# Strassen output product in a pooled-attention MLP kernel: which queue carries loads and stores, how x is normalised, and when pooling starts

## The chip, the cores and the metric

The kernel runs on one core of one Trainium2 chip. The metric is the device time of that core in microseconds. A core has TensorE (PE in the profile; its weight loads are PEld), VectorE (DVE), ScalarE (ACT), GpSimd (POOL) and SyncE (SP). SyncE, ScalarE and GpSimd can issue DMAs; the data is moved by 16 DMA engines. All engines work through their own instruction streams in order and wait for each other by semaphores.

## The reference

Attention with pooled keys and values, then an MLP without biases. Batch 8, 8 heads, 576 positions, head size 64, hence 4608 tokens of 512 features; hidden size 2048. All inputs and the output are float32.

```python
k_p = k.reshape(B, H, S // 8, 8, D).mean(axis=3)       # 72 pooled keys
v_p = v.reshape(B, H, S // 8, 8, D).mean(axis=3)
attn = softmax(q @ k_p.T / sqrt(D))
x = (attn @ v_p) as [B * S, H * D]                     # 4608 x 512
h = x @ w_in                                           # 4608 x 2048
g = h - tanh(h)
out = g @ w_out                                        # 4608 x 512
```

## The kernel before

The tokens are taken in nine groups g of 512 (TG), while the attention works in eight batches of 576 tokens. Attention runs ahead of the MLP: during group g of the MLP, the scores and the attention product of batch nb = g + 1 are computed and the inputs of batch nn = g + 2 are loaded and pooled. The order of the instructions is written out by hand; each engine executes its part in that order.

**Hidden layer of a group.** Eight steps p (`h_pair`, the last one as two `h_one`). Each multiplies xT with two 128-column slices of w_in into two PSUM banks (L538), ScalarE takes the tanh (L550), VectorE subtracts it (L551) into Gt. During these steps VectorE also forms sums of Gt, P (`sum_p`, L559) and Q (`sum_q`, L564).

**Output product of a group.** Strassen's scheme with seven products n of half-size blocks, each in two halves u (u = 0..13), accumulated in two PSUM banks, C1 = 6 and C2 = 7 (L594). Between them `after_product` copies or combines partial results: ScalarE copies C1 (L632, L638, L645), VectorE writes quarters of the output tile O (L634, L643, L648), GpSimd subtracts m4 = O − m45 (L639), and VectorE forms the differences Dg of Gt (`sum_d`, L569), which the sixth and seventh products read. The last quarter is copied after the loop (L993). O is one buffer [128, 4, 512]: tiles 0 and 1 are token rows 0..255 of the group, tiles 2 and 3 rows 256..511.

**Attention inside the output product.** Scores of batch nb at u = 0..4 (`scores`, L349, exponential L368). At u = 6, 7, 8, 9, 11 one block of 128 tokens each (`av`): per half of the heads, three matmuls (L396) into one PSUM bank, a reciprocal of the four denominators (L413), and a product (L414) into x_sb, a pool of five buffers. Banks 2 to 5, 0 and 1 take turns for this; the next group's `h_pair` uses them again, beginning with 0 and 1. x_sb is transposed into xT by DMA (L443). Blocks that belong to the next group are transposed at once, later ones (`late`) in the next group, before its output product. xT is a ring of three groups.

**Queues before the change.** SyncE's queue carries, in this order in each group: the transpose of the pooled keys (L332, at p = 0), five transposes of q (L205, each after a ScalarE cast of q, L192), the loads of batch nn (k 2 DMAs, v 5, q 2; L137 to L170), the `late` transposes of x and those of the first blocks of batch nb (L443). GpSimd's stream carries: pooling of k and v of batch nn (`pool_k`, `pool_v`, from u = 6; L248 to L291), placing the transposed keys (`k_place`), the stores of the previous group's four tiles (`store_tile`, L615, emitted at p = 0), and m4 (L639). The loads wait for buffers: k_raw and v_raw have two each, used by batches in turn; q_raw has one, free after the third ScalarE cast of the batch before.

The stores of the last group are issued after the loop on SyncE (`store`, L611); the last product is done for each of the two row tiles apart, copied to O (L1004), and stored in turn on SyncE and ScalarE (L1006). A tile of 128 rows can consist of two segments in the output, which then are two DMAs; in the last group all four tiles do.

Of the kernel before, what the change touches and what calls it, by code (L numbers as in the profile page):

```python
# [8 lines left out]
FP32 = mybir.dt.float32  # L9
# [19 lines left out]
NT = 5  # L29
# [13 lines left out]
def kernel(  # L43
# [89 lines left out]
            nc.vector.tensor_copy(out=out, in_=in_)  # L133
        evac_n[0] += 1

    def load_main(src, dst, b, t0, t1):
        return nc.sync.dma_start(out=dst[:, t0:t1, :], in_=src[b, 0:128, t0:t1, :])  # L137

    def load_left(src, dst, b, eng=nc.sync):
        return [  # L140
            eng.dma_start(out=dst[32 * t : 32 * t + LO, NM, :], in_=src[b, 128:PR, t, :])
            for t in range(NM)
        ]

    def load_dense(src, dst, b, eng=nc.sync):
        return eng.dma_start(
            out=dst[0 : NM * LO, NM, :], in_=src[b, 128:PR, :, :]
        )

    def load_k(b):  # L150
        return [
            load_main(k_pairs, k_raw[b % 2], b, 0, NM),
            load_dense(k_pairs, k_raw[b % 2], b),
        ]

    def load_v(b):
        return [load_main(v_pairs, v_raw[b % 2], b, 0, NM)] + load_left(
            v_pairs, v_raw[b % 2], b
        )

    def load_q_tail(b, t, eng):
        eng.dma_start(
            out=t[:QT, :, R, :], in_=q[b, :, QA:S, :].rearrange("h p d -> p h d")
        )

    def load_q(b, tail=True):
        if b not in q_raws:
            q_raws[b] = raw.tile([128, H, R + 1, D], FP32, name="q_raw", tag="q_raw")
        t = q_raws[b]
        nc.sync.dma_start(  # L170
            out=t[:, :, 0:R, :], in_=q[b, :, 0:QA, :].rearrange("h (p j) d -> p h j d", j=R)
        )
        if tail:
            load_q_tail(b, t, nc.sync)

    qTs = {}
    kdups = {}
# [60 lines left out]
    def halves(n, b):  # L238
        return ((0, n),) if b < 2 else ((0, n // 2), (n // 2, n))

    def pool_k(b, eng, t0=0, t1=NT, mid=()):
        r = k_raw[b % 2].rearrange("p t (j d) -> p t j d", d=D)[:, t0:t1, :, :]
        if b not in kdups:
            kdups[b] = work.tile([128, NT, 2, D], BF16, name="kd", tag="kd")
        kd = kdups[b][:, t0:t1, :, :]
        n = t1 - t0
        for ta, tb in halves(n, b):
            first = eng.tensor_tensor(  # L248
                out=r[:, ta:tb, 0:4, :], in0=r[:, ta:tb, 0:4, :], in1=r[:, ta:tb, 4:8, :], op=ALU.add
            )  # L250
        for c in mid:
            load_w2(c)
        eng.tensor_tensor(  # L253
            out=r[:, :, 0:2, :], in0=r[:, :, 0:2, :], in1=r[:, :, 2:4, :], op=ALU.add
        )
        eng.tensor_tensor(  # L256
            out=kd,
            in0=r[:, :, 0:1, :].to_broadcast([128, n, 2, D]),
            in1=r[:, :, 1:2, :].to_broadcast([128, n, 2, D]),
            op=ALU.add,  # L260
        )
        return first
# [158 lines left out]
    def new_x():  # L421
        return work.tile([128, 2, 4, D], BF16, name="x_sb", tag="x_sb", bufs=5)

    def av(b, blk, alloc, by_dma):
        x_sb = new_x()
        for half in range(2):
            av_half(b, blk, half, x_sb, alloc)
        if by_dma:
            if b * S + blk * 128 < (b + 1) * TG:
                x_dma_transpose(b, blk, x_sb)  # L430
            else:
                late.append((b, blk, x_sb))
        return x_sb
# [132 lines left out]
        )  # L566

    def sum_d(a, b):
        nc.vector.tensor_tensor(  # L569
            out=Dg[:, a:b, :, :],  # L570
            in0=Gt[:, a:b, :, 0:HT],
            in1=Gt[:, a:b, :, HT:TG],
            op=ALU.subtract,
        )
# [28 lines left out]
    def chain(g, bk):  # L603
        if g == NG - 1 and bk == C1:
            return PS[:, 2:4, 0:HD]
        return PS[:, bk, :].rearrange("p (t n) -> p t n", t=2)

    def store(g, th, c0=0, c1=DM):
        for tt in range(2):
            for r0, r1, dst in out_segments(g * TG + th * HT + tt * 128, 128):  # L610
                nc.sync.dma_start(out=dst[:, c0:c1], in_=O[r0:r1, 2 * th + tt, c0:c1])  # L611

    def store_tile(g, tb):
        for r0, r1, dst in out_segments(g * TG + tb * 128, 128):
            nc.gpsimd.dma_start(out=dst, in_=O[r0:r1, tb, :])  # L615

    def sh(c, off):
        return slice(c.start + off, c.stop + off)
# [8 lines left out]
        (C1, lambda k, c: Dg[:, k, 1, c], w2s[:, 2, :, :]),  # L627
    ]

    def after_product(g, n):  # L630
        if n == 0:
            nc.scalar.copy(out=m4, in_=chain(g, C1))  # L632
        if n == 1:
            nc.vector.tensor_tensor(out=O[:, 2:4, 0:HD], in0=chain(g, C2), in1=m4, op=ALU.add)  # L634
            sum_d(0, 2)
            sum_d(2, 4)
        if n == 2:
            nc.scalar.copy(out=m45, in_=chain(g, C1))  # L638
            nc.gpsimd.tensor_tensor(out=m4, in0=O[:, 2:4, 0:HD], in1=m45, op=ALU.subtract)  # L639
            sum_d(4, 6)  # L640
            sum_d(6, 8)
        if n == 3:
            nc.vector.tensor_tensor(out=O[:, 0:2, HD:DM], in0=m4, in1=chain(g, C2), op=ALU.subtract)  # L643
        if n == 4:
            nc.scalar.copy(out=m451, in_=chain(g, C1))  # L645
            nc.vector.tensor_tensor(out=m451, in0=m451, in1=m45, op=ALU.subtract)
        if n == 5:
            nc.vector.tensor_tensor(  # L648
                out=O[:, 2:4, HD:DM], in0=m451, in1=chain(g, C2), op=ALU.subtract
            )  # L650
# [288 lines left out]
    for g in range(1, NG):  # L939
        nb = g + 1 if g + 1 < B else None  # L940
        nn = g + 2 if g + 2 < B else None
        for p in range(NP - 1):
            c = p if g > 1 else p - 1
            if nb is not None and 0 <= c < 3:
                q_cast_part(nb, c)
            h_pair(g, p, (0, 2, 4, 6, 0, 2, 4)[p], p % 2)
            if g == 1 and p < 4:
                w_sum(w2s[:, 0, :, :], b11, b22, ALU.add, k0=2 * p, k1=2 * p + 2)
            if 3 <= p < 6:
                sum_p(2 * p - 6, 2 * p - 4)  # L950
            if nb is not None and p == 0:
                k_dma_transpose(nb)
                k_place(nb, nc.gpsimd.tensor_copy)
            if g > 1 and p == 0:
                for tb in range(4):
                    store_tile(g - 1, tb)
            if nb is not None and 0 <= c < 3:
                q_dma_transpose(nb, 2 * c, min(2 * c + 2, R + 1))
            if nb is not None and c == 2:
                if nn is not None:  # L960
                    load_k(nn)
                    load_v(nn)
                    load_q(nn)
        h_one(g, NP - 1, 1, 0, 2)
        h_one(g, NP - 1, 0, 1, 3)
        sum_p(6, 8)
        sum_q(0, 4)
        sum_q(4, 8)
        while late:
            x_dma_transpose(*late.pop(0))  # L970
        ps_a = Banks(2, 3, 4, 5, 0, 1)
        for u in range(14):
            n, half = u // 2, u % 2
            bk, lhs, rhs = products[n]
            if n == 6 and g == NG - 1:
                break
            product(g, bk, lhs, rhs, 4 * half, 4 * half + 4, n < 2)
            if half:
                after_product(g, n)
                if g == 1 and n in (1, 2):  # L980
                    w_sum(w2s[:, 2, :, :], b21, b22, ALU.add, k0=4 * n - 4, k1=4 * n)
            if nb is not None:
                if u < NT:
                    scores(nb, u)
                if u == NT:
                    ps_a.n += 2
                if u in (6, 7, 8, 9, 11):
                    av(nb, (6, 7, 8, 9, 11).index(u), ps_b1, True)
                if u == 6 and nn is not None:
                    pool_k(nn, nc.gpsimd)  # L990
                    pool_v(nn, nc.gpsimd)
        if g < NG - 1:
            nc.scalar.copy(out=O[:, 0:2, 0:HD], in_=chain(g, C1))  # L993
    store(NG - 1, 1)
    store(NG - 1, 0, c0=HD)
    bk, lhs, rhs = products[6]
    for tt in range(2):
        product(NG - 1, bk, lhs, rhs, 0, NP, False, (tt,))
        for c0, c1, eng in (
            ((0, HD, nc.scalar.copy),)  # L1000
            if tt == 0
            else ((0, HD // 2, nc.scalar.copy), (HD // 2, HD, nc.vector.tensor_copy))
        ):
            eng(out=O[:, tt, c0:c1], in_=part(NG - 1, C1, tt, c0, c1))  # L1004
        for n, (r0, r1, dst) in enumerate(out_segments((NG - 1) * TG + tt * 128, 128)):
            (nc.sync, nc.scalar)[n % 2].dma_start(out=dst[:, 0:HD], in_=O[r0:r1, tt, 0:HD])  # L1006


# [28 lines left out]
```

The softmax here doesn't subtract the row's maximum and nothing guards it: scores larger than these inputs give would overflow.

## Time and profile before

Three runs: 298.72, 299.71 and 300.87 us; median 299.71. The profiled execution has a span of 300.0 us and a mean granted TensorE clock of 0.988.

| engine | busy us | share of the span |
|---|---|---|
| TensorE, matmul | 281.9 | 94% |
| TensorE, weight load | 179.0 | 60% |
| VectorE | 227.6 | 76% |
| ScalarE | 153.6 | 51% |
| GpSimd | 146.1 | 49% |

How to read it: TensorE's hidden layer and output products are the body of the time, about 29 us for a group; the first group ends at about 56 us, since weights and the first batch must be loaded and prepared. Groups begin their hidden layer at 56.0, 87.25, 118.9, 149.9, 180.5, 209.9, 239.1 and 265.2 us. In the lines of the profile, a row of 40 digits divides the span in slices of 7.5 us; each digit is the busy share in tenths (in the clock row, the granted clock). A wait line tells which engine at which line waited for what, with total, number and longest. A timeline line has start, duration, engine, line, operation, tiles and count; where several instructions are merged, the duration is from the first start to the last end.

### The profile page before, as it was taken

How to read it: one execution, taken by the hardware profiler on the slowest of the kernel's cores; microseconds unless marked ns; L12 is line 12 of the kernel's file. 1: busy time of each engine (PE TensorE's matmuls, PEld its weight loads, DVE VectorE, ACT ScalarE, POOL GpSimd, SP SyncE). 2: the span in 40 equal slices, each digit the busy share in tenths (PEclk: the TensorE clock that was granted, in tenths of full speed). 3: DMA queues.
4: the chain of work that ended last, by engine and by line, in shares of the span. 5: the costliest groups of instructions: out<-in, count | busy, mean ns of one | idle time of the engine just before them, and what ended most of it. 6: DMA issues, size and time to landing. Idle time of an engine off the chain costs nothing.

```text
span 300.0 us, 5470 instructions
## 1 busy us (share of the span) xinstructions
PE 281.9 (94%) x2040; PEld 179.0 (60%) x2040; DVE 227.6 (76%) x400; ACT 153.6 (51%) x244; POOL 146.1 (49%) x166
## 2 busy tenths in 40 slices
PE   7999999999989996999999999999999999999980
PEld 3454455446864685448845874489458845864870
DVE  5658675799977977498969875987898859838940
ACT  4647576586337722566086616660865155235410
POOL 8600909960599259900995199409941040130020
PEclk9999999999999999899999999999999999999997
DMA  7999999949545999399948985799483450030014
GB/s 253 220 213 281 318 236 298 256 79 323 152 86 93 307 296 90 72 267 318 101 92 240 330 125 98 218 351 117 77 184 48 71 149 2 0 120 22 0 27 116
DMA packets 64587, 49.85 MB, mean 166 GB/s; under 512 B 39984, under 2 KB 53296, under 8 KB 64560
## 3 DMA queue, kind: packets, MB, share of 16 engines
q1 hardware_dynamic: 54736, 35.60, 51.8%
q0 software_dynamic: 7248, 12.06, 17.5%
q10 hardware_dynamic: 2576, 1.84, 2.2%
q8 instruction: 16, 0.26, 0.4%
q14 instruction: 11, 0.09, 0.1%
HBM read 36.70 MB, written 9.44 MB: 154 GB/s over the span
## 4 chain that ended last, share of the span: by engine, by line
PE 76%; DMA 10%; DVE 6%; POOL 4%; ACT 1%; issue 1%; ACTq 0%; SPq 0%; POOLq 0%
PE PS L538 34%; PE PS L594 31%; DMA w1b<-in_moe_w_in_dram 4%; PE PS L396 4%; PE PS L520 4%; DMA k_raw<-in_k_dram 4%; PE PS L349 3%; DVE Gt L551 3%; DMA xT<-x_sb 2%; POOL k_raw L248 1%; DVE w2s L577 1%; DVE P L559 1%; DVE x_sb L414 1%; POOL k_raw L253 1%; POOL kd L256 1%
## 5 line engine op out<-in xcount | busy, mean ns | idle before, releaser
L538 PE MATMUL PS<-xT,w1b 128*128 128x512 bf16 x512 | 113.5, 383 | 5.2 <-DMA xT<-x_sb 3.1
L551 DVE TENSOR_TENSOR Gt<-PS,TS 128x1024 bf16<-128x1024 f32 x56 | 68.4, 1221 | 28.2 <-ACT TS L550 28.2
L538 PEld LDWEIGHTS <-w1b 128*128 128x128 f16 x512 | 50.0, 98 | 66.3 <-issue 6.8
L550 ACT ACTIVATE TS<-PS 128x1024 f32<-128x1024 f32 x56 | 57.3, 1024 | 37.2 <-PE PS L538 28.4
L639 POOL TENSOR_TENSOR m<-O,m 128x512 f32<-128x512 f32 x8 | 11.9, 1492 | 98.3 <-ACT m L638 74.7
L414 DVE TENSOR_TENSOR x_sb<-PS,rden 128x256 bf16<-128x256 f32 x72 | 30.6, 425 | 6.6 <-DMA xT<-x_sb 4.2
L594 PE MATMUL PS<-w2s,Dg 128*128 128x256 f16 x256 | 30.2, 273 | 0.0
L615 POOL DMA_DIRECT2D out_dram<-O x44 | 23.6, 545 | 13.4 <-ACT O L993 13.4
L248 POOL TENSOR_TENSOR k_raw<-k_raw 128x512 f32<-128x512 f32 (+2 forms) x13 | 22.0, 1709 | 16.6 <-DMA k_raw<-in_k_dram 16.6
L594 PEld LDWEIGHTS <-Gt 128*128 128x128 bf16 x256 | 24.4, 98 | 5.8 <-DVE Gt L556 0.5
L594 PEld LDWEIGHTS <-P 128*128 128x128 bf16 x256 | 24.5, 98 | 4.7 <-issue 1.4
L594 PEld LDWEIGHTS <-Dg 128*128 128x128 bf16 x256 | 24.5, 98 | 2.8 <-issue 0.2
L368 ACT ACTIVATE E<-PS 128x288 bf16<-128x288 f32 x60 | 21.3, 410 | 7.7 <-PE PS L349 7.6
L559 DVE TENSOR_TENSOR P<-Gt 128x1024 bf16<-128x1024 bf16 x32 | 22.0, 687 | 0.6
L569 DVE TENSOR_TENSOR Dg<-Gt 128x1024 bf16<-128x1024 bf16 x32 | 22.1, 750 | 0.0
L396 PE MATMUL PS<-VB,E 128*128 128x130 bf16 x240 | 20.2, 220 | 0.1
L645 ACT COPY m<-PS 128x512 f32<-128x512 f32 x8 | 4.7, 586 | 29.5 <-PE PS L594 29.5
L267 POOL TENSOR_TENSOR v_raw<-v_raw 128x512 f32<-128x512 f32 (+1 forms) x12 | 19.6, 1654 | 0.0
L396 PEld LDWEIGHTS <-E 128*128 128x128 bf16 x240 | 16.8, 98 | 1.9 <-issue 0.4
L349 PE MATMUL PS<-qT,KB 128*128 128x288 bf16 (+5 forms) x128 | 17.0, 289 | 0.2
L594 PE MATMUL PS<-w2s,Gt 128*128 128x256 f16 x128 | 16.7, 273 | 0.4 <-DVE Gt L556 0.2
L993 ACT COPY O<-PS 128x512 f32<-128x512 f32 x7 | 4.1, 585 | 24.6 <-PE PS L594 24.6
(109 smaller groups left out, 399.1 us busy)
## 6 DMA issues: line engine op xcount, KB each, us to landing
k_raw<-in_k_dram SPq DMA_DIRECT2D x7, 1024.0 KB, 7.3
q_raw<-in_q_dram SPq DMA_DIRECT2D x7, 1024.0 KB, 12.4
v_raw<-in_v_dram SPq DMA_DIRECT2D x7, 1024.0 KB, 11.2
out_dram<-O POOLq DMA_DIRECT2D x32, 128.0 KB, 5.6
out_dram<-O POOLq DMA_DIRECT2D x12, 256.0 KB, 3.6
w1b<-in_moe_w_in_dram POOLq DMA_DIRECT2D x4, 512.0 KB, 14.1
w2b<-in_moe_w_out_dram POOLq DMA_DIRECT2D x4, 512.0 KB, 16.7
out_dram<-O SPq DMA_DIRECT2D x4, 256.0 KB, 4.5
```

The lines of the kernel that those rows point to most:

```text
L248: first = eng.tensor_tensor(out=r[:, ta:tb, 0:4, :], in0=r[:, ta:tb, 0:4, :], in1=r[:, ta:tb, 4:8, :], op=ALU.add)
L349: nc.tensor.matmul(dst[p : p + w], lhsT=KB[b % 2][:, o : o + w], rhs=qTs[b][:, m, c0:c1], start=True, stop=True,)
L368: nc.scalar.activation(out=E[:, t, half * hs : (half + 1) * hs], in_=ps[:, :], func=ACT.Exp, scale=SCALE)
L396: nc.tensor.matmul(ps[:, 2 * n : 2 * n + 2, :].rearrange("p h d -> p (h d)") if n < 2 else ps.rearrange("p (a s) d -> p a s d", s=2)[:, :, ...
L414: nc.vector.tensor_tensor(out=x_sb[:, half, :, :], in0=ps[:, :, 0:D], in1=rden[:, :, :].to_broadcast([128, 4, D]), op=ALU.mult,)
L538: nc.tensor.matmul(dst, lhsT=w1b[:, fb, i * 128 : (i + 1) * 128], rhs=xT[:, fb, c0 : c0 + TG], start=(fb == 0), stop=(fb == NFB - 1),)
L550: nc.scalar.activation(out=t2, in_=PS[:, b0 : b0 + 2, :], func=ACT.Tanh)
L551: nc.vector.tensor_sub(out=Gt[:, p, :, :], in0=PS[:, b0 : b0 + 2, :], in1=t2)
L559: nc.vector.tensor_tensor(out=P[:, a:b, :], in0=Gt[:, a:b, 0, :], in1=Gt[:, a:b, 1, :], op=ALU.add)
L569: nc.vector.tensor_tensor(out=Dg[:, a:b, :, :], in0=Gt[:, a:b, :, 0:HT], in1=Gt[:, a:b, :, HT:TG], op=ALU.subtract,)
L594: nc.tensor.matmul(part(g, bk, tt), lhsT=lhs(k, slice(tt * 128, (tt + 1) * 128)), rhs=rhs[:, k, :], start=(first and k == 0 and (tt == 0 o ...
L615: nc.gpsimd.dma_start(out=dst, in_=O[r0:r1, tb, :])
```

## The change

The change redistributes work between queues and engines; what is computed stays the same.

1. The loads of batch nn in the group loop are issued by GpSimd in place of SyncE.
2. `store_tile` is issued by SyncE in place of GpSimd, tiles 2 and 3 at p = 0 (ahead of the transposes of q), tiles 0 and 1 at p = 3 (behind them).
3. `av_both` normalises both halves of a block at once, over two PSUM banks, with one reciprocal and one product where there were two of each.
4. m4 = O − m45 moves from GpSimd to VectorE and from after the third product to after the fourth.
5. All four `sum_d` follow the second product, and the first instruction of `pool_k` on GpSimd waits for the last of them (`gate`), so that pooling and the differences don't run at the same time.
6. In the last group the two output quarters that are ready after the fourth product are stored then; the third is stored on SyncE and GpSimd; the two row tiles of the last quarter are copied by ScalarE and VectorE, one each, and stored on ScalarE's and SyncE's queues.

```diff
-    def load_main(src, dst, b, t0, t1):
-        return nc.sync.dma_start(out=dst[:, t0:t1, :], in_=src[b, 0:128, t0:t1, :])
+    def load_main(src, dst, b, t0, t1, eng=nc.sync):
+        return eng.dma_start(out=dst[:, t0:t1, :], in_=src[b, 0:128, t0:t1, :])
...
-    def pool_k(b, eng, t0=0, t1=NT, mid=()):
+    def pool_k(b, eng, t0=0, t1=NT, mid=(), dep=None):
...
+            if dep is not None and ta == 0:
+                after([first], dep)
...
+    def av_both(b, blk, x_sb):
+        b0 = ps_a.ids[ps_a.n % len(ps_a.ids)]
+        ps_a.n += 2
+        ps = PS[:, b0 : b0 + 2, 0 : 4 * D1].rearrange("p k (h d) -> p k h d", d=D1)
+        for half in range(2):
+            av_mms(b, blk, half, ps[:, half, :, :])
+        rden = work.tile([128, 2, 4, 1], FP32, name="rden2", tag="rden2")
+        nc.vector.reciprocal(out=rden[:, :, :, :], in_=ps[:, :, :, D:D1])
+        nc.vector.tensor_tensor(
+            out=x_sb[:, :, :, :],
+            in0=ps[:, :, :, 0:D],
+            in1=rden[:, :, :, :].to_broadcast([128, 2, 4, D]),
+            op=ALU.mult,
+        )
...
-        for half in range(2):
-            av_half(b, blk, half, x_sb, alloc)
+        if by_dma:
+            av_both(b, blk, x_sb)
+        else:
+            for half in range(2):
+                av_half(b, blk, half, x_sb, alloc)
...
-    def store(g, th, c0=0, c1=DM):
+    def store(g, th, engs, c0, c1):
         for tt in range(2):
             for r0, r1, dst in out_segments(g * TG + th * HT + tt * 128, 128):
-                nc.sync.dma_start(out=dst[:, c0:c1], in_=O[r0:r1, 2 * th + tt, c0:c1])
+                engs[tt].dma_start(out=dst[:, c0:c1], in_=O[r0:r1, 2 * th + tt, c0:c1])
 
     def store_tile(g, tb):
         for r0, r1, dst in out_segments(g * TG + tb * 128, 128):
-            nc.gpsimd.dma_start(out=dst, in_=O[r0:r1, tb, :])
+            nc.sync.dma_start(out=dst, in_=O[r0:r1, tb, :])
...
         if n == 1:
             nc.vector.tensor_tensor(out=O[:, 2:4, 0:HD], in0=chain(g, C2), in1=m4, op=ALU.add)
-            sum_d(0, 2)
-            sum_d(2, 4)
+            for k in range(0, NP, 2):
+                gate[0] = sum_d(k, k + 2)
         if n == 2:
             nc.scalar.copy(out=m45, in_=chain(g, C1))
-            nc.gpsimd.tensor_tensor(out=m4, in0=O[:, 2:4, 0:HD], in1=m45, op=ALU.subtract)
-            sum_d(4, 6)
-            sum_d(6, 8)
         if n == 3:
+            nc.vector.tensor_tensor(out=m4, in0=O[:, 2:4, 0:HD], in1=m45, op=ALU.subtract)
             nc.vector.tensor_tensor(out=O[:, 0:2, HD:DM], in0=m4, in1=chain(g, C2), op=ALU.subtract)
+            if g == NG - 1:
+                store(g, 1, (nc.sync, nc.sync), 0, HD)
+                store(g, 0, (nc.sync, nc.sync), HD, DM)
...
-            if g > 1 and p == 0:
-                for tb in range(4):
+            if g > 1 and p in (0, 3):
+                for tb in (2, 3) if p == 0 else (0, 1):
                     store_tile(g - 1, tb)
...
-                    load_k(nn)
-                    load_v(nn)
-                    load_q(nn)
+                    load_k(nn, nc.gpsimd)
+                    load_v(nn, nc.gpsimd)
+                    load_q(nn, eng=nc.gpsimd)
...
-                    pool_k(nn, nc.gpsimd)
+                    pool_k(nn, nc.gpsimd, dep=gate[0])
                     pool_v(nn, nc.gpsimd)
...
-    store(NG - 1, 1)
-    store(NG - 1, 0, c0=HD)
+    store(NG - 1, 1, (nc.sync, nc.gpsimd), HD, DM)
     bk, lhs, rhs = products[6]
-    for tt in range(2):
+    for tt, eng in ((0, nc.scalar.copy), (1, nc.vector.tensor_copy)):
         product(NG - 1, bk, lhs, rhs, 0, NP, False, (tt,))
-        for c0, c1, eng in (
-            ((0, HD, nc.scalar.copy),)
-            if tt == 0
-            else ((0, HD // 2, nc.scalar.copy), (HD // 2, HD, nc.vector.tensor_copy))
-        ):
-            eng(out=O[:, tt, c0:c1], in_=part(NG - 1, C1, tt, c0, c1))
+        eng(out=O[:, tt, 0:HD], in_=part(NG - 1, C1, tt))
         for n, (r0, r1, dst) in enumerate(out_segments((NG - 1) * TG + tt * 128, 128)):
-            (nc.sync, nc.scalar)[n % 2].dma_start(out=dst[:, 0:HD], in_=O[r0:r1, tt, 0:HD])
+            (nc.scalar if tt == 0 or n else nc.sync).dma_start(
+                out=dst[:, 0:HD], in_=O[r0:r1, tt, 0:HD]
+            )
```

`load_k`, `load_v` and `load_q` pass the issuing engine on in the same way as `load_main`.

More of the change, by code (lines that the diff above doesn't have):

```diff
@@ L148, in load_dense, with load_k, load_v @@
         )
-    def load_k(b):
+    def load_k(b, eng=nc.sync):
         return [
-            load_main(k_pairs, k_raw[b % 2], b, 0, NM),
-            load_dense(k_pairs, k_raw[b % 2], b),
-        ]
-    def load_v(b):
-        return [load_main(v_pairs, v_raw[b % 2], b, 0, NM)] + load_left(
-            v_pairs, v_raw[b % 2], b
+            load_main(k_pairs, k_raw[b % 2], b, 0, NM, eng),
+            load_dense(k_pairs, k_raw[b % 2], b, eng),
+        ]
+    def load_v(b, eng=nc.sync):
+        return [load_main(v_pairs, v_raw[b % 2], b, 0, NM, eng)] + load_left(
+            v_pairs, v_raw[b % 2], b, eng
         )
@@ L164, in load_q_tail, with load_q @@
         )
-    def load_q(b, tail=True):
+    def load_q(b, tail=True, eng=nc.sync):
         if b not in q_raws:
@@ L169, in load_q @@
         t = q_raws[b]
-        nc.sync.dma_start(
+        eng.dma_start(
             out=t[:, :, 0:R, :], in_=q[b, :, 0:QA, :].rearrange("h (p j) d -> p h j d", j=R)
@@ L173, in load_q @@
         if tail:
-            load_q_tail(b, t, nc.sync)
+            load_q_tail(b, t, eng)
     qTs = {}
@@ L568, in sum_d @@
     def sum_d(a, b):
-        nc.vector.tensor_tensor(
+        return nc.vector.tensor_tensor(
             out=Dg[:, a:b, :, :],
@@ L628 @@
     ]
+    gate = [None]
     def after_product(g, n):
```

## The prediction

> **What bounds the kernel now.** I read the page first: the slices of busy time, then the chain of work that ended last.
>
> ```profile
> span 300.0 us, 5470 instructions
> PE   7999999999989996999999999999999999999980
> PEclk9999999999999999899999999999999999999997
> DMA  7999999949545999399948985799483450030014
> PE 76%; DMA 10%; DVE 6%; POOL 4%; ACT 1%; issue 1%; ACTq 0%; SPq 0%; POOLq 0%
> ```
>
> TensorE is nearly full in all but a few slices, so only its holes can be won back: the slices before 120 us, one slice (120 to 127.5 us) with a lower clock, and the last one. PE's waits between 72 and 290 us and the stretches around 118 us show what these are:
>
> ```profile
> PE PS L538 <- DMA xT<-x_sb: 3.1, 2, 2.3
> PE PS L538 <- DVE x_sb L414: 1.2, 1, 1.2
> 116.64:118.92 2.28, 0.00 (x0) 0.03 (x1) 1.86 (x6) 1.53 (x2) 2.28 (x3) 0.94 0.60 118
> 118.92:120.00 1.08, 1.08 (x3) 0.40 (x4) 0.71 (x3) 0.00 (x0) 1.08 (x1) 0.50 0.73 143
> 120.00:121.00 1.00, 1.00 (x3) 0.29 (x2) 0.00 (x0) 0.00 (x0) 0.92 (x2) 0.50 0.67 131
> 121.00:122.00 1.00, 1.00 (x4) 0.43 (x3) 0.00 (x0) 0.00 (x0) 0.92 (x2) 0.50 0.55 108
> ```
>
> Columns of the last four: stretch, length, busy time of PE, PEld, DVE, ACT, POOL, granted clock, DMA share, GB/s. Three waits stand at the start of a group: 0.86 us at 87.25 (group 2), 2.28 us at 118.92 (group 3), 1.24 us at 180.53 (group 5). After the 2.28 us the clock is 0.50 until 122: group 3's hidden layer takes 15.51 us by the chain, where groups 2 and 4 take 13.99 and 13.97. That makes 1.53 us.
>
> Why is xT late? SyncE's queue, in order of time, in group 2:
>
> ```profile
> 96.10 0.58 SPq L137 DMA_DIRECT2D k_raw<-in_k_dram  x1
> 98.00 2.94 SPq L141 DMA_DIRECT2D v_raw<-in_v_dram  x4
> 100.99 0.55 SPq L170 DMA_DIRECT2D q_raw<-in_q_dram  x1
> 103.76 1.48 SPq L162 DMA_DIRECT2D q_raw<-in_q_dram  x1
> 105.36 12.18 SPq L443 DMA_TRANSPOSE xT<-x_sb  x5
> DMA to landing us min/median/max: 11.5/11.5/11.5
> ```
>
> The loads of the batch after next stand ahead of the transposes of x. The first transpose issued behind them holds SyncE for 4.46 us and lands after 11.5 us, against 2.5 us for one on a quiet queue. Its x_sb buffer therefore comes free late (VectorE's L414 waits 1.0 us for it at 117), and the transpose that group 3 needs is issued at 116.33 though VectorE finished its block at 114.7. It lands at 118.8. Group 5 is the same: the first transpose takes 4.44 us to issue, the piece that the group needs goes at 176.5 and lands 3.8 us later, 180.3. So I read the wait "DVE x_sb L414" at 180.53 as this DMA; a copy happens to end at the same moment.
>
> The end, SyncE's queue and the final scalar line:
>
> ```profile
> 290.45 5.49 SPq L611 DMA_DIRECT2D out_dram<-O  x8
> 296.04 1.17 SPq L1006 DMA_DIRECT2D out_dram<-O  x2
> 292.29 0.51 ACTq L1006 DMA_DIRECT2D out_dram<-O  x1
> ```
>
> The last copy of results ends at 292.26, yet the span lasts to 300.0: eight stores at 0.69 us of issue each stand in one queue ahead of the last two, and the last issue (297.21) needs 2.8 us more.
>
> **What the Trainium skill says.** "DMA: Bandwidth & Descriptors", section Issuing engines are not separate DMA queues: all issuers share the same 16 DMA engines, several issuers save issue time only; its section Queues, rings and completion order adds that an engine takes turns between rings and works through one in order. The 11.5 us landing behind loads agrees with in-order rings; no row of before shows a transpose beside loads on another ring. "SBUF — State Buffer", section SBUF: two separate sides: a GpSimd operation and a VectorE operation with two SBUF inputs exclude each other for a whole instruction. L646 agrees: 0.69 us in the groups without pooling, 0.95 to 2.00 us beside it. "TensorE: Matmul & The Clock Gate", Part 1: the clock halves after an idle window of about 3.4 us. Here 2.28 us was enough, 0.86 and 1.24 us were not.
>
> **The change part by part.**
>
> *Stores at the end.* The eight stores of L611 become twelve, of which eight leave the tail: four (O[2:4], left half) need only L634, done at 283.5, and four (O[0:2], right half) need L643, some 287.3, since the subtraction before it now runs on VectorE (0.69 us there at 288.44) and not on GpSimd (2.01 us, with VectorE waiting 1.16 us). Eight issues of 0.69 from 284 on, the last four from 287.3, are done by 290.1. After L648 (290.42) SyncE has two of the last four (to 291.8) and GpSimd two (0.54 each). The last block is one VectorE copy of 256 elements, 0.43 us like L414, from 291.67 to 292.1; its two stores go at once on SyncE and ScalarE (ScalarE's two earlier ones end at 292.2) and are issued by 292.75. With the same 2.8 us the end is 295.5: **4.5 us less**. Bounds: 3.5 if GpSimd's two land as slowly as its 5.6 us median, 5.0 if nothing queues.
>
> *Loads to GpSimd, stores to SyncE.* GpSimd loses five to eight stores a group (0.54 each, 2.7 to 4.3 us) and L639 (1.5), and gains nine loads. A load's issue is bounded by the 128-row stores, 0.54, and the 512 KB v_raw load, 1.00; I take 0.55 for six small ones and 1.1 for three large: 6.6 us. It stands some 8 us into the group, where the stores stood (95.26, 157.87); behind it is only the next pooling, 12 us later. Its issue costs nothing. The bytes are the same, so what is won is order: the late transposes of x now wait behind stores, not loads, are issued some 12 us into the group instead of 17 to 18, and land by +17 even at the 6.3 us which is the worst landing of a qT transpose. x_sb buffers are free long before they are needed. The store that VectorE's L634 waited 1.55 us for at 106.64 goes about 6 us earlier too.
> Group 5 then starts without a wait: **1.24 us less**. Group 3: VectorE ends block 2 at about 114.4, the transpose goes at 114.7 and lands 2.46 later, 117.15, against PE's end at 116.64: a wait of 0.4 to 0.5, **1.85 us less**, and too short for the clock, **1.53 us less**.
>
> *The price on SyncE.* In groups 2 to 8 two to four stores (0.6 each) go ahead of the five transposes of q. These were done by +9 and the scores need them at +14.9: a delay of 1.2 to 2.4 us fits in the slack of 3 to 5, except that the last ones now run beside the loads. Landing 2.5 (quiet) to 6.3 (worst): +10.5 plus those is +13 to +16.8, so a wait between 0 and 2 us in groups 2 to 5. I take 0.2 each, **0.8 us more**.
>
> *Two-bank normalisation.* Per block two reciprocals (0.17) and two products (0.43), 1.10 us from start to start of blocks, become one reciprocal of 8 (L823, 0.20) and one product of 512 (L824, 0.69), 0.89: 0.2 us less on VectorE, 1.0 per group. It hides beside PE except where the last immediate block decides (groups 2 and 3).
>
> *Subtraction to VectorE, pooling gated.* VectorE gains 0.69 to 2.0 per group, like L646, ahead of L643, ahead of blocks 1 and 2, and of the sixth product, which reuses bank 7: L643 would end 205.3 ± 0.7 in group 5 and the product begins at 205.85. At worst 0.15 us; I take 0.3 in all. The gate makes GpSimd wait for the last difference (202.0 in group 5), which is 1.2 us before its pooling begins today (203.17, behind L639): no loss, and the differences run alone at 0.6 us each. At group 2's start VectorE is the limit: block 2 ends 1.2 later for the subtraction and 0.6 earlier for the pairs, and the transposes follow at 1.2 us each: **0.4 us more**.
>
> Sum: 4.5 + 1.24 + 1.85 + 1.53 − 0.8 − 0.3 − 0.4 = 7.6 us less, 299.71 − 7.6 = **292.1 us**.
>
> **Rivals.**
> All waits gone: the three gaps (4.38), the clock (1.53) and the tail (4.5) give 289.3. For it: groups 6 and 7 already follow without a gap; against it: group 2 is bound by VectorE.
> Contention instead of order: the transposes, now taking turns with loads, land as late as before, and only the tail is won: 299.71 − 4.5 + 0.5 = 295.7. For it: the DMA rows stand at 9 around these times.
> Slower: the scores' transposes of q are held by the loads as those of x were (11.5 instead of 2.5, 9 us less a slack of 4, in four groups, with 1.5 us of halved clock each): 26 − 4.5 more, 321; at a third of it, 304. The same comes if VectorE's paired sums lock GpSimd out of writing its loads, so pooling waits for k. Against it: the transposes of q go mostly before the loads, and GpSimd's stores kept 0.54 us beside these sums.
>
> **How the numbers follow.** 0.6 for my forecast (290.5 to 294.5), 0.15 for all waits gone, 0.17 for tail only, 0.08 for slower. The range runs from just under the floor, 288.5, to tail only with a weak tail and a few short score waits, 297.3. Below 296.7 (1%): 0.86; within: 0.07; above: 0.07.
>
> **What would show it.** The end: SyncE issues eight stores before the last products, and the span ends about 3 us after the last issue. The transposes of x after the scores land in under 6 us; VectorE's waits for xT are gone; the clock stays at full in group 3; L646's new neighbour takes 0.7 to 2.0 us. Wrong: a PE wait at the scores (L349) of a microsecond or more in groups 2 to 5, q transposes landing after 8 us, GpSimd pooling that waits for k_raw, or a gap over 2 us at group 2.

## The result and the profile after

The changed kernel takes 313.56 us against 299.71 us for the kernel before: 13.8 us more, a ratio of 1.046 with a 95% interval of 1.037 to 1.055. The forecast was 292.1, with a range of 288.5 to 297.3. It was wrong in direction.

Executions of one kernel spread by some per cent (the changed kernel's four from 313.24 to 318.48 us), so the medians, ratios and differences below are of those within 1.5% of a kernel's fastest, and three profiles of longer executions show only what stands where, not how large a difference is: stores back on GpSimd (322.2 us), late x transposes ahead of the loads (299.8 us) and stores behind the q transposes (304.5 us).

The profiled execution has a span of 311.7 us. Its page, the same rows as those shown of before:

```profile
span 311.7 us, 5363 instructions
PE   7999899999899289798999698989999999999994
PEclk9999999999999969999999999999999999999998
DMA  7999999869168930589637992799356135004014
PE 52%; DMA 15%; DVE 3%; issue 2%; ACT 1%
```

TensorE has a new hole of almost a whole slice (the digit 2, 101 to 109 us) and further dents near 145, 175 and 206 us, and the clock digit falls to 6 after the large one. In the chain, DMA went from 10% to 15%. Which DMA it is stands in TensorE's waits between 72 and 311 us (waiting engine, line, what it waited for; total us, times, longest):

```profile
PE PS L351 <- DMA qT<-q_bf: 12.3, 4, 6.6
PE PS L614 <- DVE O L663: 2.8, 5, 1.2
PE PS L558 <- DVE x_sb L434: 1.5, 1, 1.5
PE PS L558 <- DMA xT<-x_sb: 1.5, 2, 0.8
```

The first line did not exist before: the scores (L351, once L349) wait for the transposed q in four groups. The second is new too; it stands at L663, directly behind the subtraction that VectorE took over. The last two are the waits at the start of groups 2, 3 and 5: 0.68, 1.54 and 0.83 us, 3.05 in all, where they were 4.38. The wait for q has a price beyond its length; stretches of group 2 (columns as in the stretches of before):

```profile
103.30:109.98 6.68, 0.04 (x1) 0.00 (x0) 2.88 (x5) 0.41 (x1) 0.00 (x0) 0.89 1.08 292
109.98:115.00 5.02, 5.02 (x24) 3.48 (x24) 0.00 (x0) 2.04 (x6) 0.00 (x0) 0.50 0.31 66
```

6.7 us of nothing, then 5.0 us at half clock, hence another 2.5 us. From the timeline, group 2 now lasts 40.88 us (first hidden matmul to first hidden matmul) where it lasted 31.67; groups 1, 3, 4 and 5 lose 1.5, 0.4, 3.1 and 2.2 us, groups 6 and 7, beside which nothing is loaded, are the same to 0.01 us, and the stretch after the last matmul shrinks from 8.56 to 4.38 us. Sum: +16.4 for groups 1 to 5, −4.2 at the end, −0.5 elsewhere: the 11.7 us between the two spans.

Why q is late is seen by laying two queues beside each other. SyncE's, then GpSimd's, then the landing of the four q transposes issued from 93.2 us on (the time from issue to the arrival of the data):

```profile
88.43 3.41 SPq L635 DMA_DIRECT2D out_dram<-O  x4
91.94 6.83 SPq L205 DMA_TRANSPOSE qT<-q_bf  x5
98.82 2.92 SPq L635 DMA_DIRECT2D out_dram<-O  x4
101.78 3.31 SPq L463 DMA_TRANSPOSE xT<-x_sb  x2
...
94.48 0.81 POOL L137 DMA_DIRECT2D k_raw<-in_k_dram  x1
95.81 0.77 POOL L137 DMA_DIRECT2D v_raw<-in_v_dram  x1
98.55 0.96 POOL L170 DMA_DIRECT2D q_raw<-in_q_dram  x1
...
DMA to landing us min/median/max: 2.5/9.6/12.4
```

Four stores hold back the first transpose to 91.94; GpSimd begins its loads at 94.48, when two of the five transposes are out. The remaining three land after 7.2, 12.0 and 12.4 us. The last q transpose of groups 3, 4 and 5 lands after 9.8, 9.6 and 9.0 us. Before, the loads stood in the same queue and could not start until the fifth transpose was issued: that order was free, and it was what protected q.

### The profile page after: what moved, and what is told of

Its sections match the earlier page's. It is cut to its first block, busy times and chain, and to the rows that moved or that the text cites. A ratio compares the mean times of both kernels' runs of the same rounds, so it can differ in the third digit from the quotient of the medians.

```text
span 311.7 us, 5363 instructions
## 1 busy us (share of the span) xinstructions
PE 283.0 (91%) x2021; PEld 180.0 (58%) x2040; DVE 230.6 (74%) x348; ACT 154.0 (49%) x243; POOL 142.2 (46%) x161
## 3 DMA queue, kind: packets, MB, share of 16 engines
q0 software_dynamic: 10016, 22.55, 29.1%
q10 hardware_dynamic: 2656, 1.90, 2.2%
## 4 chain that ended last, share of the span: by engine, by line
PE 52%; DMA 15%; DVE 3%; issue 2%; ACT 1%
PE PS L614 25%; PE PS L558 23%; DMA qT<-q_bf 13%; PE PS L351 2%; PE PS L398 2%; DMA xT<-x_sb 2%; DVE O L663 1%; DVE x_sb L434 1%; DVE m L669 1%; ACT TS L570 1%; DVE rden L433 0%; DVE O L671 0%; DVE O L1021 0%
## 5 line engine op out<-in xcount | busy, mean ns | idle before, releaser
L558 PE MATMUL PS<-xT,w1b 128*128 128x512 bf16 x496 | 111.1, 379 | 5.0 <-DVE x_sb L434 1.5
L631 POOL DMA_DIRECT2D out_dram<-O x2 | 1.1, 574 | 73.8 <-DVE O L671 73.8
L351 PE MATMUL PS<-qT,KB 128*128 128x288 bf16 (+5 forms) x128 | 18.4, 296 | 12.4 <-DMA qT<-q_bf 12.3
L614 PEld LDWEIGHTS <-P 128*128 128x128 bf16 x256 | 25.2, 100 | 5.4 <-issue 1.4
L434 DVE TENSOR_TENSOR x_sb<-PS,rden 128x512 bf16<-128x512 f32 x30 | 20.7, 692 | 1.0
L269 POOL TENSOR_TENSOR v_raw<-v_raw 128x512 f32<-128x512 f32 (+1 forms) x12 | 21.5, 1808 | 0.0
L589 DVE TENSOR_TENSOR Dg<-Gt 128x1024 bf16<-128x1024 bf16 x32 | 19.9, 684 | 0.0
L656 DVE TENSOR_TENSOR O<-PS,m 128x512 f32<-128x512 f32 x8 | 5.5, 690 | 18.1 <-ACT E L370 17.8
L398 PEld LDWEIGHTS <-E 128*128 128x128 bf16 x240 | 16.8, 98 | 1.9 <-issue 0.4
L614 PE MATMUL PS<-w2s,Gt 128*128 128x256 f16 x128 | 17.6, 282 | 0.4 <-DVE Gt L576 0.2
```

Of the source, the lines that this page charges most:

```text
L269: eng.tensor_tensor(out=r[:, ta:tb, 0:4, :], in0=r[:, ta:tb, 0:4, :], in1=r[:, ta:tb, 4:8, :], op=ALU.add)
L351: nc.tensor.matmul(dst[p : p + w], lhsT=KB[b % 2][:, o : o + w], rhs=qTs[b][:, m, c0:c1], start=True, stop=True,)
L398: nc.tensor.matmul(ps[:, 2 * n : 2 * n + 2, :].rearrange("p h d -> p (h d)") if n < 2 else ps.rearrange("p (a s) d -> p a s d", s=2)[:, :, ...
L434: nc.vector.tensor_tensor(out=x_sb[:, :, :, :], in0=ps[:, :, :, 0:D], in1=rden[:, :, :, :].to_broadcast([128, 2, 4, D]), op=ALU.mult,)
L558: nc.tensor.matmul(dst, lhsT=w1b[:, fb, i * 128 : (i + 1) * 128], rhs=xT[:, fb, c0 : c0 + TG], start=(fb == 0), stop=(fb == NFB - 1),)
L589: return nc.vector.tensor_tensor(out=Dg[:, a:b, :, :], in0=Gt[:, a:b, :, 0:HT], in1=Gt[:, a:b, :, HT:TG], op=ALU.subtract,)
```

## Experiments

Three theories run through the expectations. A ring here is the list from which the DMA engines take the transfers of one issuing engine; the profile counts them as q1 (SyncE), q0 (GpSimd) and q10 (ScalarE). Theory R says that the loads hurt because they are on a ring of their own beside the transposes. Theory S says that the stores ahead push the transposes into them. Theory V puts the loss on VectorE.

**Loads back on SyncE.**

```diff
-load_k(nn, nc.gpsimd); load_v(nn, nc.gpsimd); load_q(nn, eng=nc.gpsimd)
+load_k(nn); load_v(nn); load_q(nn)
```

> The changed kernel with the loads of batch nn back on SyncE's queue (behind the q transposes there), all else as changed. Theory R (rings): the changed kernel loses because the last two q transposes run beside the loads on GpSimd's ring; then they land in about 2.5 us again, the waits of TensorE at L351 (12.3 us) and the halved clock after them go, and the time is before less the 4.0 us of the tail, plus 1 to 3 us for VectorE's extra subtraction: 297 to 299 us. Theory V (VectorE: subtraction and gate are the cost): the time stays above 305 us.

Measured: 298.52 us (ratio to before 0.994, 0.990 to 0.997). One edit takes back 15.0 us, more than the 13.8 lost, and no wait at L351 is left; q transposes land in 4.0 us at most. V falls as the main cause. TensorE's largest wait is now this one:

```profile
PE PS L614 <- DVE O L663: 3.5, 4, 1.9
```

**No loads in the group loop.** In place of the three loads, `q_raws[nn] = q_raws[nb]`: the kernel leaves the loads out and computes the later batches on old data.

> The changed kernel without the loads of k, v and q in the group loop: attention from the fourth batch on works on old data. It shows what the changed kernel costs beside the collision of DMAs. If the collision is all of the loss: transposes land in 2.5 us, no waits at L351 or for xT, and what is left is the tail (4.0 less), the three gaps and the clock (up to 5.9 less), plus VectorE's waits at L663 (2.8 us): 292 to 294 us. If VectorE or the gate has a share of the loss: above 297 us.

Measured: 296.53 us (0.990, 0.983 to 0.997), between the two numbers expected and far from the changed kernel. All q transposes land in 2.6 us. The loads, with all that they do to other DMAs, thus account for 17.0 us of the changed kernel (313.56 − 296.53). It also bounds the rest: with no loads to collide with, the whole change is worth some 3 us against the kernel before, no more than the tail alone (below). In place of the gaps that I counted on winning TensorE waits for VectorE, 1.6 us at L663 and 1.6 at x_sb, and 1.0 us for xT.

**Only the new tail**, on the kernel before (stores and copies of the last group, as in the diff above).

> The kernel before with only the new stores and copies of the last group. Both theories: the span ends 4.4 us after TensorE instead of 8.4, nothing else moves, 4.0 us less than before: 296 us. If the tail gain were tied to the subtraction on VectorE, under 3 us.

Measured: 296.13 us, ratio 0.984 (0.979 to 0.990), 3.9 us less. The tail's gain needs none of the other parts.

**Stores back on GpSimd**, ahead of the loads.

```diff
-            nc.sync.dma_start(out=dst, in_=O[r0:r1, tb, :])
+            nc.gpsimd.dma_start(out=dst, in_=O[r0:r1, tb, :])
...
-            if g > 1 and p in (0, 3):
+            if g > 1 and p == 0:
```

> The changed kernel with store_tile back on GpSimd, all four at p = 0, ahead of the loads there; loads stay on GpSimd. It moves the q transposes 1 to 3.5 us earlier and the loads 2.7 to 4.3 us later. Theory S (the stores ahead on SyncE are what pushes the q transposes into the loads): no overlap is left, L351 waits under 1 us, 295 to 298 us. Theory R in its strict form (loads on a ring of their own hurt whatever is beside them): the late x transposes, now beside the loads, take over as the wait at the group starts: 300 us or more.

Measured: 311.4 to 330.3 us in four executions, too wide a spread to rank it against the changed kernel, but slower than the kernel before. Theory S's 295 to 298 is far off, and theory R's strict form (300 or more) holds. GpSimd now issues two things in one line: the q load goes out at 105.87 in group 2 (98.55 in the changed kernel). ScalarE's casts of q follow late: in group 5 the first waits 3.7 us for the q load, the five q transposes stretch over 12.2 us from 185.83 on (6.9 us in the changed kernel), and those that meet the loads issued from 192.99 on land after up to 20.9 us. The longest wait at L351 is 12.1 us. This run moved both sides and so did not separate S from R.

**First load gated behind the last q transpose**, loads on GpSimd.

```diff
-                    load_k(nn, nc.gpsimd)
+                    after(load_k(nn, nc.gpsimd)[:1], last_qt[0])
...
-            nc.sync.dma_start_transpose(
+            last_qt[0] = nc.sync.dma_start_transpose(
```

> The changed kernel with the first load of each batch (k) waiting for the last q transpose to land; GpSimd keeps the loads, SyncE the stores. Theory R: all q transposes land in 2.5 us, L351 doesn't wait, and what is left is the gain of the tail and of free x_sb buffers less VectorE's price: 294 to 298 us. Theory V: above 305 us. If loads that start 2 to 3 us later come too late for pooling, GpSimd shows a wait for k_raw at L248 beyond the one at the start.

Measured: 309.55 us (1.031, 1.024 to 1.038). q is cured, and the wait moves to the next thing that SyncE transposes. TensorE's first waits, and the landing of the two late x transposes issued from 99.9 us:

```profile
PE PS L559 <- DMA xT<-x_sb: 8.2, 3, 6.0
PE PS L559 <- DVE x_sb L435: 3.8, 1, 3.8
...
DMA to landing us min/median/max: 12.8/15.6/18.4
```

These two transposes now stand beside GpSimd's loads, and land after 12.8 and 18.4 us.

**Gate, and the late x transposes ahead of it.** In addition to the edit above:

```diff
-                nc.sync.dma_start_transpose(
+                last_qt[0] = nc.sync.dma_start_transpose(
...
             if nb is not None and c == 2:
+                while late:
+                    x_dma_transpose(*late.pop(0))
```

> The changed kernel (loads on GpSimd, stores on SyncE) with the late transposes of x ahead, and the first load gated behind the landing of the last of them. Theory Q: with nothing small beside the loads until the first attention block, q transposes and late x transposes land in 2.5 us; loads begin 5 us later than in the changed kernel and run into the first x transposes of the output product, so the wait moves there: 300 to 306 us. If it were only the q and late x transposes that matter: 294 to 296 us.

Measured: 305.99 us (one execution); waits for xT at group starts total 8.1 us in four. As theory Q (what a transpose stands behind or beside sets its landing) expected, the collision moves on to the first x transposes of the output product: in group 2 they land after 6.9 to 10.9 us, and the next group starts 5.45 us late. None of the places tried so far for a group's 3.5 MB of loads was free; what could be chosen was whom they meet.

**Loads on ScalarE's queue**, to see whether it is GpSimd's ring in particular.

```diff
-load_k(nn, nc.gpsimd)
+load_k(nn, nc.scalar)          # v and q likewise
```

> The changed kernel with the loads of batch nn on ScalarE's queue, a hardware ring, in place of GpSimd's. The reading is the landing of the transposes that run beside them, not the time: ScalarE issues nine loads in the middle of the hidden layer and holds up its tanh for 5 to 8 us a group, so 310 to 330 us. Theory P (turns go by packet, GpSimd's packets are large, 3.4 KB on average against 0.22 KB of a transpose): packets of 1.7 KB take half as long per turn, and a transpose beside them lands in 5 to 7 us. Theory A (any other ring holds it as much): 9 to 12 us as on GpSimd's.

Measured: 368.97 us (one execution). Much worse than expected, since TensorE waits 62.3 us for Gt: ScalarE's tanh stands behind DMA issues that wait (in group 2 the k load is issued at 103.55, the next at 111.05). The reading is in the packets of the rings while transposes (q1) and loads (q0 or q10) are both under way; columns: packets, MB, share of 16 engines. First the changed kernel, 101 to 108 us; then this one, 105 to 108 us and 108 to 110 us; then the changed kernel at 92 to 94 us, without loads (559 small packets of transposes and 69 larger ones of a store):

```profile
q0 software_dynamic: 610, 2.04, 94.4%
q1 hardware_dynamic: 607, 0.15, 13.1%
...
q10 hardware_dynamic: 375, 0.77, 84.8%
q1 hardware_dynamic: 9, 0.00, 0.2%
...
q1 hardware_dynamic: 1107, 0.26, 102.0%
q10 hardware_dynamic: 132, 0.24, 31.3%
...
DMA packets 628, 0.27 MB, mean 136 GB/s; under 512 B 559, under 2 KB 559, under 8 KB 628
```

Without loads, 280 transpose packets pass per us, with the engines 62% busy, so this is no ceiling. Beside GpSimd's loads it is 87 per us, and as many load packets: 607 against 610, and so too within most single microseconds (92 to 91, 146 to 144, 78 to 81, 63 to 64, 81 to 80, 78 to 79). The run with the gate shows it again, 448 to 454 from 106 to 112 us. So the two rings take turns by packet, one to one, and the turns are unequal: estimated from the shares, a load packet (3.3 KB on average) holds an engine for 0.17 us and a transpose packet (0.25 KB) for 0.024 us. A transpose has some 580 packets (2326 for four, with nothing beside them, at 239 to 252 us): 6.7 us each at 87 per us, and more for one queued behind others. Not every stretch is like this: from 170 to 173 us only 30 transpose packets pass beside 228 of loads, which no run explains.

Beside ScalarE's loads the rings don't alternate in this way. From 105 to 108 us 9 transpose packets pass beside 375 of loads, though q transposes are under way; in the next two microseconds it is 1107 beside 132. The landing is shorter than beside GpSimd's loads: at most 7.2 us in groups 2 and 3, where theory P expected 5 to 7, and 9.0 in group 1. But without turns one by one theory P's reason, the size of the load packets, is not shown.

**Stores behind the q transposes**, loads where the change put them. This separates S from R.

```diff
-            if g > 1 and p in (0, 3):
-                for tb in (2, 3) if p == 0 else (0, 1):
+            if g > 1 and p == 3:
+                for tb in (2, 3, 0, 1):
```

> The changed kernel with all four store_tile at p = 3 on SyncE, behind the q transposes, in place of two ahead and two behind; loads stay on GpSimd and start when they did. The q transposes go 1 to 3.4 us earlier. Theory S (the delay is the cause): the q transposes are through before the loads, no wait at L351, 297 to 299 us. Theory R (the loads' own ring is the cause): one or two transposes fewer stand beside the loads, the others still land in 7 to 12 us, the late x transposes go later by as much; L351 waits 2 to 8 us in place of 12.3, 305 to 312 us.

Measured: 296.72 us, ratio 0.988 (0.985 to 0.991): theory S's number, 16.8 us below the changed kernel, for a shift of two to four stores past five transposes. SyncE in group 2, and the landing of the q transposes issued from 93 to 97 us:

```profile
89.50 7.53 SPq L205 DMA_TRANSPOSE qT<-q_bf  x5
97.11 8.91 SPq L635 DMA_DIRECT2D out_dram<-O  x8
106.29 16.34 SPq L463 DMA_TRANSPOSE xT<-x_sb  x5
...
DMA to landing us min/median/max: 2.5/3.6/9.7
```

The loads begin at 94.70, as before the edit, and a transpose that meets them still lands in 9.7 us: R's mechanism is there. But it is only the last one, issued at 95.8, and the scores wait 2.0 us for it in this profile, instead of 6.6. Both theories are needed: the rings make the landing long, the stores decide how many transposes pay it. What stands beside the loads is now the stores (97.11 to 106.02); the late x transposes come after the last load is issued (101.97) and land in 7.7 us at most. So loads on GpSimd's ring need not be slower than on SyncE's: with them back on SyncE it was 298.5 us.

**VectorE's part.** On the version with loads on SyncE, the subtraction m4 was moved in two ways: on VectorE straight after the third product, with pooling gated behind it, and back on GpSimd.

```diff
         if n == 2:
             nc.scalar.copy(out=m45, in_=chain(g, C1))
+            gate[0] = nc.vector.tensor_tensor(out=m4, in0=O[:, 2:4, 0:HD], in1=m45, op=ALU.subtract)
         if n == 3:
-            nc.vector.tensor_tensor(out=m4, in0=O[:, 2:4, 0:HD], in1=m45, op=ALU.subtract)
```

> Loads back on SyncE (298.5 us before this edit), and the subtraction m4 on VectorE right after the third product, ahead of the first attention block, with pooling gated behind it in place of the last difference. Theory L (the subtraction costs because GpSimd's pooling holds the shared port when it starts: 2.3 us in place of 0.7): it takes 0.7 us, the waits of TensorE at L663 (3.5 us) go, 295 to 296 us. If its place in VectorE's stream alone is the cost: no change, 298 us.

> Loads back on SyncE, and m4 back on GpSimd after the third product (behind the gated pooling's place in program order, ahead of it in the stream). Theory L and its rival agree on fewer waits at L663: 295 to 297 us; the two-bank normalisation and the stores on SyncE then show what they are worth against the kernel before with only the tail, 296.1 us.

Measured: 298.61 us (0.996, 0.993 to 0.999) and 299.69 us (1.001, 0.999 to 1.003). The subtraction itself behaves as theory L said. In the changed kernel, and moved ahead of pooling (min/median/max ns):

```profile
L662 DVE TENSOR_TENSOR m<-O,m x8: 681/1868/2287, 81.4 to 301.8; 128x512 f32<-128x512 f32 x8
...
L661 DVE TENSOR_TENSOR m<-O,m x8: 684/692/693, 79.3 to 286.2; 128x512 f32<-128x512 f32 x8
```

But the time did not fall: another wait took its place. VectorE, in the version with m4 early:

```profile
DVE O L663 <- DMA out_dram<-O: 11.3, 4, 4.9
```

In the version with only the loads on SyncE this wait was 1.6 us; TensorE's wait at L663 went from 3.5 to 4.6 us. L663 overwrites tiles 0 and 1 of O, whose stores of the group before now stand behind the loads on SyncE (in group 2 of the version with loads on SyncE they are issued from 104.58 us on, behind a q load issued at 103.85). With loads and stores in one queue, the stores are what is late. My expectation of 295 to 297 us missed this.

**Parts on the kernel before, with the new tail.** Two-bank normalisation alone; then with all differences at once, m4 early on VectorE and pooling gated behind it.

> The kernel before with the new tail and the two-bank normalisation, nothing else. By VectorE's durations (0.89 in place of 1.10 us a block) 1 us a group is saved on VectorE; where the last block decides the next group's start (groups 2 and 3) up to 0.6 us each: 295 to 296 us. If waiting for both banks costs TensorE more than it saves VectorE: 296.5 to 297.5 us.

> The kernel before with the new tail, the two-bank normalisation, all differences at once, m4 on VectorE straight after the third product and pooling gated behind it; loads on SyncE, stores on GpSimd, order as before. Against tail_av (296.3 us) it tells what VectorE's part is worth: 295 to 296 us if running the sums apart from pooling gains the 0.3 to 0.6 us that they lose beside it; 296.5 to 298 us if the gate delays pooling and the subtraction delays the attention blocks by more.

Measured: 296.28 us (0.984, 0.979 to 0.989) and 295.85 us (0.990, 0.984 to 0.996), both within half a microsecond of the tail alone. VectorE's part costs nothing measurable once m4 stands ahead of pooling, and wins nothing that these executions can tell.

**Late x transposes ahead of the loads**, both on SyncE, stores on GpSimd, new tail; then with VectorE's part.

```diff
+                while late:
+                    x_dma_transpose(*late.pop(0))
                 if nn is not None:
                     load_k(nn)
```

> The kernel before with the new tail (296.1 us), and the late transposes of x issued on SyncE ahead of the loads in place of behind them; loads and stores on their old queues. Theory Q (what a transpose stands behind or beside on the DMA engines sets its landing): the late transposes land in under 4 us, x_sb buffers are free, the gaps ahead of groups 3 and 5 (2.2 us and 1.2 us beyond 29.2 and 30.4 us a group) go: 293 to 295 us. If VectorE and not the transposes limits those groups: 296 us.

> The same (late transposes ahead of the loads, new tail, loads on SyncE, stores on GpSimd) with the changed kernel's two-bank normalisation, all four differences at once, and m4 on VectorE straight after the third product with pooling gated behind it. If VectorE's part of the change is worth something where no DMA is late: 1 to 2 us below late_first. If its price and gain cancel: within 0.7 us of late_first.

Measured: 297.49 us (0.992, 0.989 to 0.996) and 297.27 us (0.994, 0.990 to 0.998), no better than the tail alone (0.984). Theory Q's 293 to 295 is missed. In the first version's group 2 the late transposes land after 4.7 to 6.0 us, not under 4; the loads start 3.4 us later than with the tail alone (99.11 against 95.72), nearer to the first x transposes of the output product; and TensorE waits for xT 7.1 us in four groups:

```profile
PE PS L538 <- DMA xT<-x_sb: 7.1, 4, 3.1
```

In the profile of the second version, of an execution of 295.5 us, this wait is 1.8 us in two groups. How much of the miss is due to it is therefore not shown.

The fastest versions tried are the kernel before with the new tail, with or without VectorE's part (295.9 to 296.3 us), and the changed kernel with its stores behind the q transposes (296.7 us); their intervals overlap.

## Why the prediction was wrong

**The tail was right.** Predicted 4.5 us; 4.2 in the changed kernel's trace, 3.9 measured alone.

**The step that failed is "The price on SyncE".** The start time was right: the last q transpose was put at +10.5 us and is issued at +9.2 in group 2. The landing was not: "landing 2.5 (quiet) to 6.3 (worst)" took the worst landing of a q transpose in the trace of before, beside a few stores, as the bound beside 3.5 MB of loads. Measured for the last q transpose of groups 2 to 5 are 9.0 to 12.4 us; in group 2 the transposes' small packets got one turn for each load packet of GpSimd's ring (607 to 610 packets). So "0.2 each, 0.8 us more" is 12.3 us of waiting at L351 plus some 2.5 us of half clock in group 2. I had the right number in front of me, 11.5 us for a transpose behind these loads, and put it into the rival "Slower" with 0.08; the outcome, 313.6, lies between that rival's two sizes, 304 and 321. The argument given against it, that the transposes of q go mostly before the loads, was an assumption on order where the change had removed the order: in one queue the loads followed the transposes by construction, on two they follow only if they happen to be later.

**"Its issue costs nothing" was right and beside the point.** GpSimd issues the nine loads of group 2 in 5.8 us (0.81 + 0.53 + 0.77 + 1.98 + 0.96 + 0.70) plus one wait of 2.0 us, near the 6.6 estimated, and pooling never waited for k. What counts is when the loads start, not what they cost to issue.

**The x transposes.** They were to land "by +17 even at 6.3 us". In group 2 the two issued at 101.8 and 103.5 land after 9.9 and 8.5 us, at +23.3 and +23.6. The wait before group 3 came out at 1.54 us, not 0.4 to 0.5, and that before group 5, which was to vanish, at 0.83 us (1.24 before).

**VectorE's price was mis-sized.** "At worst 0.15 us; I take 0.3 in all": measured are 2.8 us of TensorE's waits for L663. The likely reason is that m4 beside pooling takes up to 2.29 us (median 1.87), where L646 had suggested 0.69 to 2.0, and stands directly ahead of L663; no run takes this wait alone away. m4's length agrees with what the Trainium skill ("SBUF — State Buffer", section SBUF: two separate sides) says on the port that VectorE and GpSimd hold in turn: moved ahead of pooling, it takes 0.69 us in all eight groups. With m4 there, the gated pooling costs nothing that the kernel before with the new tail and VectorE's part shows (295.85 us).

**On the clock**, 1.53 us were to be saved in group 3. They were (its hidden layer takes 13.97 us), and 2.5 us were lost in group 2, after a longer gap.

What stays open: how the 17.0 us of collision divide between waits for q, for x and the clock; holding the loads back until q has landed leaves 309.6 us, while moving the stores out of q's way leaves 296.7 us. The one-to-one turns are counted beside GpSimd's ring only. Whether packet size or another property of the ring makes the landing shorter beside ScalarE's loads is open; no run changed the size on one ring.

## What to carry to other kernels

A queue is also an order: before moving a transfer to a second queue, list what it used to be unable to overtake, and price those as if they ran beside it for as long as it runs. Small-packet transfers (DMA transposes) are the ones that lose beside bulk loads, so keep them ahead of the loads in one queue, or let the loads run beside transfers that nothing waits for soon (here the stores: 296.7 us). Making the loads wait moved the collision to the next transposes in line (309.6 us). Stores that end a kernel are worth spreading over queues and issuing as soon as each part is ready: here 3.9 us, the only one of the six parts for which a gain was measured. The loads and the stores were not moved one at a time on the kernel before.

## What the runs showed of the hardware

- Beside GpSimd's loads, SyncE's transposes get one packet for each load packet (607 to 610 in 7 us, 448 to 454 in 6 us of another run), and their rate falls from 280 to 87 packets per us. The Trainium skill ("DMA: Bandwidth & Descriptors", section Queues, rings and completion order) says that an engine takes turns between rings at packet granularity; these counts agree. Beside ScalarE's loads no such alternation is seen (9 to 375 in 3 us, then 1107 to 132 in 2 us).
- The same data has larger packets when GpSimd issues it: the five batches of loads in the group loop make 5,200 packets on GpSimd's ring (10,016 of the changed kernel less 4,816 without those loads) and 14,160 on ScalarE's (16,816 less 2,656), for 17.7 MB each: 3.4 KB against 1.25 KB.
- A gap of 6.7 us on TensorE was followed by 5.0 us at half clock; one of 2.28 us in the kernel before already cost 3 us at half clock.
